# Routing attention and MLP on one core: attention of all sequences as one part, the MLP as a second, steps in pairs

## The chip, the core and the metric

The kernel runs on one core of a Trainium2 chip. The metric is the time of one execution on the device in microseconds. A core has TensorE (PE: matmuls, and PEld: its weight loads), VectorE (DVE), ScalarE (ACT), GpSimd (POOL) and SyncE (SP), which here only issues transfers. Each engine takes the instructions of its own queue in order and waits on semaphores for the others.

## What is computed

Two blocks follow each other. The first is attention with routing, for 4 sequences of 768 tokens and 8 heads of 64: each query and key goes to the nearest of 16 centroids of its head, and a query sees only keys of its own centroid. The second is an MLP on rows of 512 (the 8 heads side by side) with a layer norm and a residual.

```python
q_assign = np.argmax(np.einsum('bhsd,hcd->bhsc', q_n, c_n), axis=-1)
k_assign = np.argmax(np.einsum('bhsd,hcd->bhsc', k_n, c_n), axis=-1)
mask = q_assign[:, :, :, None] == k_assign[:, :, None, :]
scores = np.where(mask, scale * np.matmul(q, k.transpose(0, 1, 3, 2)), -1000000000.0)
attn = softmax(scores)          # over the keys
x = np.matmul(attn, v)          # heads side by side: (4, 768, 512)
...
xn = (x - mu) / np.sqrt(var + 1e-06) * g_ln
out = x + np.maximum(xn @ w_ch1, 0.0) @ w_ch2     # 512 -> 2048 -> 512
```

The two weight matrices come as float64; the kernel turns them into float32 on the chip.

## The kernel before, in words

Two heads make a pair; 4 sequences of 4 pairs give 16 pairs `n`. A pair has two halves `g` of 384 queries and six key tiles `c` of 128: 12 steps of (pair, half, key tile), 192 in all.

One step is `scores` and `weigh`. `scores` (L300) computes, for both heads, the product of the one-hot centroid tiles in bf16 (L307, keys scaled so that a mismatch gives a huge negative number) and adds the float32 product of keys and queries (L312); the heads use different row halves of the array. ScalarE takes the exponential into one of four `e` tiles (L317). `weigh` (L320) multiplies `e` with V, each head on its own column half, and adds over the six key tiles in one PSUM tile (L327). A float32 matmul shows as two instructions in the trace. The sums of `e` over the key tiles, for the denominators, are five additions a half: GpSimd two (L339, L341), VectorE three (L339, L343, L344).

A pair is prepared while the one before it is in its steps: transposes of q and k (L232, copies at L238 and L240), similarities to the centroids (L250, twelve matmuls with q or k as the stationary tile and 32 columns each), routing on VectorE (L260 to L273), and transposes of the one-hot tiles (L285, copies at L291).

`finish` (L350) closes a half in three parts, 2, 5 and 9 steps after it: part 0 copies the accumulator to `xT` and sums the denominators over partitions by a matmul with ones (L361), copies them (L365) and spreads two rows over 64 partitions each by a transfer (L367); part 1 takes the reciprocal (L372), writes it to DRAM (L374) and reads it back broadcast (L377); part 2 multiplies on GpSimd (L384).

The weights come in 32 chunks of 128 x 512 float64 (16 of each matrix), with two buffers. `split_weight` (L176) has ScalarE scale the low words (L184) and VectorE rebuild the high words in five operations (L186 to L197); `join_weight` multiplies and adds on GpSimd (L204, L205). After four chunks of the first matrix `center_w1` subtracts the mean over rows (L212 on TensorE, L216 on VectorE). Chunks of the first matrix begin every fourth step from step 0, those of the second every step from step 64.

The MLP of a sequence is cut into units: for each of two halves of rows, 16 `hidden` (four matmuls of 384 columns and a ReLU: L417, L425), three `rows` (transposes L401, copies, statistics L406) and `project` (48 matmuls of 512 columns, L434; VectorE scales and adds the residual, L445; store at L449). From step 70 on a budget gains 78 a step and pays 48 for a unit, which is then put among the steps; the units of the last sequence come after all steps. So the attention of sequences 1 to 3 stands interleaved with the MLP of 0 to 2.

The program writes this order down in Python; the framework then orders each engine's queue from it, by priority and readiness in a schedule of its own, and adds the waits. All loads and stores of the loop are on SyncE's queue.

A last part tests that all reciprocals lie in a safe range; where they don't, a slow general path (not run here) computes all again.

## Time and profile before

| | us |
|---|---|
| median of 3 runs | 1256.71 (1255.5 to 1257.78) |
| the profiled execution | 1256.49 |
| its span in the trace | 1254.7 |
| TensorE busy | 1176.9 |
| VectorE busy | 373.0 |
| ScalarE busy | 337.5 |
| GpSimd busy | 251.5 |

The span is from the first to the last instruction in the trace; the execution's own time has 1.8 us more. A busy time is the union of an engine's instructions; for TensorE it says nothing of how full the array is, nor at which clock it ran, so the granted clock (PEclk, 1.00 for 2.4 GHz, 0.50 for 1.2) is read beside it. Durations in the trace overlap a little where instructions follow each other; the chain of waits gives each stretch of time to one of them.

### The profile page before, as it was taken

To read this page: it belongs to the slowest core of one execution; us is meant where nothing else is said; L and a number is where in the kernel's file an instruction comes from. 1 tells how busy PE (TensorE), PEld (TensorE's weight loads), DVE (VectorE), ACT (ScalarE), POOL (GpSimd) and SP (SyncE) were. 2 spreads that over 40 slices of the span, in tenths; PEclk is the share of its full clock that TensorE was granted. 3 is DMA by queue.
4 is the path that set the end of the run, shared out by engine and by line. 5 is a ranking of instruction groups with operands and counts; after the bars stand their busy time and mean duration, and the time that the engine had idled before them with its cause. 6 is when DMAs were issued, how large, how long until landed. Compare 5 with 4: busy or idle time off the path is not lost.

```text
span 1254.7 us, 11868 instructions
## 1 busy us (share of the span) xinstructions
PE 1176.9 (94%) x4738; PEld 554.8 (44%) x4738; DVE 373.0 (30%) x562; ACT 337.5 (27%) x532; POOL 251.5 (20%) x188
## 2 busy tenths in 40 slices
PE   6676766999999999999999999999999999999997
PEld 4232322444544455445444554445444443554553
DVE  6999998441221202111120021222111010100010
ACT  3333323443241233122402241142311331120110
POOL 4566766231111011101101010120101011000000
PEclk9787787999999999999999999999999999999999
DMA  7343532221011010020110101110010000000000
GB/s 179 91 134 92 129 103 66 51 51 39 13 29 39 15 26 19 24 53 1 32 27 24 32 13 28 49 33 20 7 36 8 8 7 24 15 1 17 9 9 19
DMA packets 98909, 49.31 MB, mean 39 GB/s; under 512 B 87584, under 2 KB 91680, under 8 KB 98848
## 3 DMA queue, kind: packets, MB, share of 16 engines
q1 hardware_dynamic: 98176, 48.45, 14.8%
q8 instruction: 39, 0.64, 0.2%
q14 instruction: 22, 0.18, 0.0%
q10 hardware_dynamic: 672, 0.03, 0.0%
HBM read 41.98 MB, written 6.39 MB: 39 GB/s over the span
## 4 chain that ended last, share of the span: by engine, by line
PE 82%; DVE 12%; issue 2%; DMA 1%; POOL 1%; SPq 1%; ACT 0%; DVEq 0%; POOLq 0%; ACTq 0%
PE h_ps L417 27%; PE o_ps L434 27%; PE a_ps L327 10%; PE s_ps L312 8%; PE s_ps L307 3%; PE sim_ps L250 3%; DVE ta L189 2%; DVE ta L194 2%; DVE tb L193 2%; PE den_ps L361 2%; DVE ta L186 2%; PE qk_ps L232 1%; DMA raw<-in_moe_w_ch_dram 1%; PE x_ps L401 1%; PE oh_ps L285 1%
## 5 line engine op out<-in xcount | busy, mean ns | idle before, releaser
L417 PE MATMUL h_ps<-xT,w 128*128 128x384 f32 x1024 | 346.7, 492 | 0.0
L434 PE MATMUL o_ps<-w,hT 128*128 128x512 f32 x768 | 342.7, 599 | 0.0
L417 PEld LDWEIGHTS h_ps<-xT,w 128*128 128x128 f32 x1024 | 189.7, 190 | 156.2 <-issue 34.8
L317 ACT ACTIVATE e<-s_ps 128x768 f32<-128x768 f32 x192 | 155.3, 810 | 258.2 <-PE s_ps L312 258.1
L434 PEld LDWEIGHTS o_ps<-w,hT 128*128 128x128 f32 x768 | 141.8, 190 | 187.4 <-issue 187.3
L327 PE MATMUL a_ps<-e,v_sb 128*64 128x384 f32 x768 | 177.6, 543 | 46.1 <-ACT e L317 29.3
L312 PE MATMUL s_ps<-t,t 64*128 64x384 f32 x768 | 165.6, 511 | 0.0
L425 ACT ACTIVATE hT<-h_ps 128x384 f32<-128x384 f32 x128 | 62.9, 491 | 349.5 <-PE h_ps L417 349.5
L339 POOL TENSOR_TENSOR es<-e 128x768 f32<-128x768 f32 x32 | 58.8, 1838 | 370.5 <-ACT e L317 370.5
L327 PEld LDWEIGHTS a_ps<-e,v_sb 128*64 128x64 f32 x768 | 39.8, 141 | 159.5 <-issue 55.7
L384 POOL TENSOR_TENSOR xT<-xT,rb 128x384 f32<-128x384 f32 x32 | 36.8, 1149 | 258.0 <-DMA rb<-row 254.8
L341 POOL TENSOR_TENSOR es<-es,e 128x768 f32<-128x768 f32 x32 | 60.6, 1893 | 138.7 <-ACT e L317 138.7
L372 DVE RECIPROCAL rdens<-rdens 128x6 f32<-128x6 f32 x32 | 6.0, 188 | 231.6 <-DMA rdens<-dsb 231.5
L312 PEld LDWEIGHTS s_ps<-t,t 64*128 64x128 f32 x768 | 73.8, 201 | 0.0
L445 DVE SCALAR_TENSOR_TENSOR o_sb<-o_ps,rstd,xr 128x512 f32<-128x512 f32 x24 | 18.0, 750 | 186.3 <-PE o_ps L434 177.3
L307 PE MATMUL s_ps<-m,m 64*128 64x384 bf16 x384 | 67.2, 347 | 0.1
L204 POOL TENSOR_TENSOR low<-low,tb 128x512 f32<-128x512 f32 x32 | 47.1, 1471 | 68.5 <-DVE tb L197 61.1
L307 PEld LDWEIGHTS <-m 64*128 64x128 bf16 x384 | 18.5, 93 | 93.3 <-issue 90.7
L343 DVE TENSOR_TENSOR es<-es,e 128x768 f32<-128x768 f32 x32 | 32.9, 1027 | 82.7 <-ACT e L317 82.7
L339 DVE TENSOR_TENSOR es<-e 128x768 f32<-128x768 f32 x32 | 35.2, 1101 | 52.8 <-ACT e L317 52.7
L250 PEld LDWEIGHTS sim_ps<-cT,t 128*128 128x128 f32 x384 | 47.3, 200 | 7.8 <-issue 5.0
L184 ACT ACTIVATE low<-raw 128x512 f32<-128x512 uint32 x32 | 21.8, 680 | 99.8 <-POOL w L205 81.7
(78 smaller groups left out, 676.0 us busy)
## 6 DMA issues: line engine op xcount, KB each, us to landing
raw<-in_moe_w_ch_dram SPq DMA_DIRECT2D x32, 512.0 KB, 3.9
q_sb<-in_q_dram SPq DMA_DIRECT2D x32, 192.0 KB, 3.7
k_sb<-in_k_dram SPq DMA_DIRECT2D x32, 192.0 KB, 3.3
v_sb<-in_v_dram SPq DMA_DIRECT2D x32, 192.0 KB, 3.3
rb<-row SPq DMA_DIRECT2D x64, 96.0 KB, 2.8
out_dram<-o_sb SPq DMA_DIRECT2D x24, 256.0 KB, 2.0
rdens<-dsb SPq DMA_DIRECT2D x64, 1.5 KB, 1.8
row<-rdens SPq DMA_DIRECT2D x32, 3.0 KB, 1.4
```

Of the source, the lines that this page charges most:

```text
L204: nc.gpsimd.tensor_tensor(low, low, fb, ALU.mult)
L250: nc.tensor.matmul(sv[:, c, side, :], st[side][:, c * P : (c + 1) * P], cT[:, pr, :, :].rearrange("p j c -> p (j c)"), start=True, stop=True,)
L307: nc.tensor.matmul(s[:, j, :HC], st["m", 1][rows[j], keys], st["m", 0][rows[j], cols], start=True, stop=False,)
L312: nc.tensor.matmul(s[:, j, :HC], st[1][rows[j], keys], st[0][rows[j], cols], start=False, stop=True,)
L317: nc.scalar.activation(e, s[:, :, :HC], AF.Exp, scale=SCALE)
L327: nc.tensor.matmul(acc[j * D : (j + 1) * D, :HC], loaded[n]["v"][:, c, j, :], e[:, j, :], start=(c == 0), stop=(c == NT - 1),)
L339: eng.tensor_tensor(es[c], soft.pop(i - 1), soft.pop(i), ALU.add)
L341: nc.gpsimd.tensor_tensor(es[1], es[1], soft.pop(i), ALU.add)
L384: nc.gpsimd.tensor_tensor(x, x, late.pop((n, g)), ALU.mult)
L417: nc.tensor.matmul(hp[:, :HC], w1[:, c, f * P : (f + 1) * P], xT[:, c, r * HC : (r + 1) * HC], start=(c == 0), stop=(c == NDC - 1),)
L425: nc.scalar.activation(hT, hp[:, :HC], AF.Relu)
L434: nc.tensor.matmul(op, st["hT", r, f][:, tt * P : (tt + 1) * P], w2[:, f, :], start=(f == 0), stop=(f == NFC - 1),)
```

## The change

The attention of all 16 pairs is now one part, whose pools are closed before the MLP of all four sequences runs as a second, with all eight PSUM banks and 20 hidden tiles. The four `xT` tiles stay in SBUF. The bodies of `rows`, `hidden` and `project` are the same; they are no longer cut into units.

- Steps go in pairs (slots, six to a head pair): the scores of the two steps of the next slot, then the weightings of the two of this one. There are five `e` tiles.
- Similarities: the centroids are the stationary tile, and q and k stream, 384 columns at a time, in four matmuls on four column groups of 32 (`tile_position`); ScalarE copies the result, three transposes bring it to tokens on partitions, and the routing has two operations for the one-hots where there were four.
- `finish` works on a pair: four matmuls on four column groups of 32 for the denominators, four rows to spread, one reciprocal, one trip through DRAM, one product. The accumulator of a half is copied to `xT` right behind its last weighting.
- The sums of `e` (five a half, in place), the product with the reciprocals, and all seven operations of the weight conversion are on VectorE; ScalarE's `low` and GpSimd's part are gone. A conversion has one set of work tiles. Two chunks are converted per pair, over all 16 pairs.
- The product of `mean` with g moves from ScalarE to VectorE at the start; q and k have one load buffer each, as before, and are loaded further ahead.

The diff, cut to what the text speaks of:

```diff
+    xpool = ctx.enter_context(tc.tile_pool(name="xpool", bufs=1))
...
-    loads = pool("loads", 2)
+        return stage.enter_context(tc.tile_pool(name=name, bufs=bufs, **kw))
+
+    loads = pool("loads", 1)
     heads = pool("heads", 2)
-    route = pool("route", 2)
+    route = pool("route", 1)
     attn = pool("attn", 2)
-    xpool = pool("xpool", 2)
+    conv = pool("conv", 1)
     dram = pool("dram", 4, space=bass.MemoryType.DRAM)
     ps_s = pool("ps_s", 2, space=PSUM)
     ps_a = pool("ps_a", 1, space=PSUM)
-    ps_t = pool("ps_t", 3, space=PSUM)
-    pools = {}
+    pools = {"t": pool("ps_t", 3, space=PSUM)}
...
-    ones = const.tile([P, D], F32, name="ones")
+    ones = const.tile([P, Q], F32, name="ones")
...
-        oh = const.tile([P, NT, 2, D], BF16, name=f"onehot_{side}")
+        oh = const.tile([P, TH, NHALF, 2, D], BF16, name=f"onehot_{side}")
...
-    DE = HC // D
-    rdens = const.tile([P, B * NPAIR * NHALF, DE], F32, name="rdens")
+    DE = HC // Q
+    rdens = const.tile([P, B * NPAIR, DE], F32, name="rdens")
...
-    for c in range(NDC):
-        nc.scalar.mul(mean[:, c, :], mean[:, c, :], g_sb[:, c : c + 1])
...
+    for c in range(NDC):
+        nc.vector.tensor_scalar_mul(mean[:, c, :], mean[:, c, :], g_sb[:, c : c + 1])
...
     def load_weight(m):
-        src, _ = weight_chunk(m)
-        raw = pools["conv"].tile([P, WC], mybir.dt.int64, tag="raw", name="raw")
-        nc.sync.dma_start(out=raw, in_=src)
-        raws[m] = raw
-
-    halves = {}
+        if m < NWC:
+            raw = conv.tile([P, WC], mybir.dt.int64, tag="raw", name="raw", bufs=2)
+            nc.sync.dma_start(out=raw, in_=weight_chunk(m)[0])
+            raws[m] = raw
...
     def split_weight(m):
-        words = raws.pop(m).bitcast(U32).rearrange("p (n w) -> p n w", w=2)
-        lo, hi = words[:, :, 0], words[:, :, 1]
-        cpool = pools["conv"]
-        ta = cpool.tile([P, WC], U32, tag="ta", name="ta")
-        tb = cpool.tile([P, WC], U32, tag="tb", name="tb")
-        fa, fb = ta.bitcast(F32), tb.bitcast(F32)
-        low = cpool.tile([P, WC], F32, tag="low", name="low")
-        nc.scalar.activation(low, lo, AF.Copy, scale=2.0 ** -52)
+        words = raws[m].bitcast(U32).rearrange("p (n w) -> p n w", w=2)
+        hi = words[:, :, 1]
+        ta = conv.tile([P, WC], U32, tag="ta", name="ta")
+        tb = conv.tile([P, WC], U32, tag="tb", name="tb")
...
-
         nc.vector.tensor_single_scalar(tb, hi, 0x7FF00000, op=ALU.bitwise_and)
+        halves[m] = (ta, tb)
+
+    def join_weight(m):
+        lo = raws.pop(m).bitcast(U32).rearrange("p (n w) -> p n w", w=2)[:, :, 0]
+        ta, tb = halves.pop(m)
+        fa, fb = ta.bitcast(F32), tb.bitcast(F32)
+
         nc.vector.scalar_tensor_tensor(
             out=fa, in0=tb, scalar=float(0x38100000), in1=fa, op0=ALU.is_ge, op1=ALU.mult
         )
+
         nc.vector.tensor_single_scalar(tb, ta, 0xFF800000, op=ALU.bitwise_and)
-        halves[m] = (fa, fb, low)
-
-    def join_weight(m):
-
-        _, dst = weight_chunk(m)
-        fa, fb, low = halves.pop(m)
-        nc.gpsimd.tensor_tensor(low, low, fb, ALU.mult)
-        nc.gpsimd.tensor_tensor(dst, low, fa, ALU.add)
+        nc.vector.scalar_tensor_tensor(
+            out=fb, in0=lo, scalar=2.0 ** -52, in1=fb, op0=ALU.mult, op1=ALU.mult
+        )
+        nc.vector.tensor_tensor(weight_chunk(m)[1], fb, fa, ALU.add)
...
+    def prep_sims(n):
+
...
         sim = ps("sim_ps")
-        sv = sim[:, : NG * NCL].rearrange("p (t s c) -> p t s c", s=2, c=2 * NCL)
-        for c in range(NT):
-            for side in range(2):
+        for side in range(2):
+            for g in range(NHALF):
+                r = (side * NHALF + g) * Q
                 nc.tensor.matmul(
-                    sv[:, c, side, :],
-                    st[side][:, c * P : (c + 1) * P],
+                    sim[r : r + Q, :HC],
                     cT[:, pr, :, :].rearrange("p j c -> p (j c)"),
+                    prepared[n][side][:, g * HC : (g + 1) * HC],
                     start=True,
                     stop=True,
-                )
-        sims = sim[:, : NG * NCL].rearrange("p (g c) -> p g c", c=NCL)
+                    tile_position=(0, r),
+                )
+        sim_sb = route.tile([P, HC], F32, tag="sim", name="sim_sb")
+        nc.scalar.copy(sim_sb, sim[:, :HC])
+        prepared[n]["sim"] = sim_sb
+
+    def prep_route(n):
+        sim_sb = prepared[n]["sim"]
+        simT = ps("simT_ps")
+        for c in range(TH):
+            nc.tensor.transpose(
+                simT[:, c * P : (c + 1) * P], sim_sb[:, c * P : (c + 1) * P], ident
+            )
...
-        first = route.tile([P, NT, 2, 2], F32, tag="first", name="first")
-        nc.vector.tensor_reduce(first.rearrange("p t s j -> p (t s j)"), hit, AX.X, ALU.max)
-        revs = rev.unsqueeze(1).to_broadcast([P, NT, NCL])
+        first = route.tile([P, TH, 2, NHALF * 2], F32, tag="first", name="first")
+        nc.vector.tensor_reduce(first.rearrange("p c s a -> p (c s a)"), hit, AX.X, ALU.max)
+        shape = [P, TH, NHALF * 2, NCL]
 
         for side, op in ((0, ALU.is_equal), (1, ALU.not_equal)):
-            for j in range(2):
-                nc.vector.tensor_tensor(
-                    onehots[side][:, :, j, :NCL],
-                    revs,
-                    first[:, :, side, j].unsqueeze(2).to_broadcast([P, NT, NCL]),
-                    op,
-                )
+            nc.vector.tensor_tensor(
+                onehots[side].rearrange("p c g j d -> p c (g j) d")[:, :, :, :NCL],
+                rev.unsqueeze(1).unsqueeze(1).to_broadcast(shape),
+                first[:, :, side, :].unsqueeze(3).to_broadcast(shape),
+                op,
+            )
...
-    x_of = {}
...
+    xT = [xpool.tile([P, NDC, S], F32, name=f"xT{b}") for b in range(B)]
...
-        e = attn.tile([P, 2, HC], F32, tag="e", name="e", bufs=4)
+        e = attn.tile([P, 2, HC], F32, tag="e", name="e", bufs=5)
...
-        es = sums.setdefault((n, g), {})
-        if c == 1 or c == 3:
-            es[c] = attn.tile([P, 2, HC], F32, tag=f"es{c}", name=f"es{c}")
-            eng = nc.gpsimd if c == 1 else nc.vector
-            eng.tensor_tensor(es[c], soft.pop(i - 1), soft.pop(i), ALU.add)
-        elif c == 4:
-            nc.gpsimd.tensor_tensor(es[1], es[1], soft.pop(i), ALU.add)
-        elif c == 5:
-            nc.vector.tensor_tensor(es[3], es[3], soft.pop(i), ALU.add)
-            nc.vector.tensor_tensor(es[3], es[3], es[1], ALU.add)
+        if c == 1:
+            es = attn.tile([P, 2, HC], F32, tag="es", name="es", bufs=3)
+            sums[n, g] = es
+            nc.vector.tensor_tensor(es, soft.pop(i - 1), soft.pop(i), ALU.add)
+        elif c > 1:
+            es = sums[n, g]
+            nc.vector.tensor_tensor(es, es, soft.pop(i), ALU.add)
+        if c == NT - 1:
+            b, pr = pairs[n]
+            nc.scalar.copy(xT[b][:, pr, g * HC : (g + 1) * HC], accs.pop((n, g))[:, :HC])
...
-    def finish(n, g, part):
+    def finish(n, part):
...
         if part == 0:
-            if b not in x_of:
-                x_of[b] = xpool.tile([P, NDC, S], F32, tag="x", name="xT")
-            nc.scalar.copy(x_of[b][:, pr, cols], accs.pop((n, g))[:, :HC])
-            es = sums.pop((n, g))[3]
             den = ps("den_ps")
             for j in range(2):
-                nc.tensor.matmul(
-                    den[j * D : (j + 1) * D, :HC], ones, es[:, j, :], start=True, stop=True
-                )
-            dsb = attn.tile([P, HC], F32, tag="dsb", name="dsb")
-            nc.scalar.copy(dsb[: D + 1, :], den[: D + 1, :HC])
-            for j in range(2):
-                nc.sync.dma_start(
-                    out=rdens[j * D : (j + 1) * D, r, :],
-                    in_=dsb[j * D : j * D + 1, :],
-                )
+                for g in range(NHALF):
+                    r = (j * NHALF + g) * Q
+                    nc.tensor.matmul(
+                        den[r : r + Q, :HC], ones, sums[n, g][:, j, :],
+                        start=True, stop=True, tile_position=(0, r),
+                    )
+            dsb = attn.tile([P, HC], F32, tag="dsb", name="dsb", bufs=1)
+            nc.scalar.copy(dsb, den[:, :HC])
+            for r in range(0, P, Q):
+                nc.sync.dma_start(out=rdens[r : r + Q, n, :], in_=dsb[r : r + 1, :])
         elif part == 1:
-            nc.vector.reciprocal(rdens[:, r, :], rdens[:, r, :])
-            row = dram.tile([2, HC], F32, tag="row", name="row")
-            nc.sync.dma_start(out=row.rearrange("j (p e) -> (j p) e", e=DE), in_=rdens[:, r, :])
-            rb = attn.tile([P, HC], F32, tag="rb", name="rb")
+            nc.vector.reciprocal(rdens[:, n, :], rdens[:, n, :])
+            row = dram.tile([2, S], F32, tag="row", name="row")
...
+            rb = attn.tile([P, S], F32, tag="rb", name="rb", bufs=1)
...
                 nc.sync.dma_start(
                     out=rb[j * D : (j + 1) * D, :],
-                    in_=row[j : j + 1, :].to_broadcast([D, HC]),
-                )
-            late[n, g] = rb
+                    in_=row[j : j + 1, :].to_broadcast([D, S]),
+                )
+            late[n] = rb
         else:
-            x = x_of[b][:, pr, cols]
-            nc.gpsimd.tensor_tensor(x, x, late.pop((n, g)), ALU.mult)
...
+            x = xT[b][:, pr, :]
+            nc.vector.tensor_tensor(x, x, late.pop(n), ALU.mult)
...
-    prep = {
-        0: lambda n: prep_transpose(n, 0),
-        2: lambda n: prep_transpose(n, 1),
-        4: prep_route,
-        9: prep_onehot,
-    }
-    for s in sorted(prep):
-        prep[s](0)
-    load(1, "qk")
-    work = deque()
-    pools["ffn"] = pool("ffn", 2)
-    conv = fast.enter_context(ExitStack())
-    pools["conv"] = conv.enter_context(tc.tile_pool(name="conv", bufs=2))
...
-    begin = {4 * m if m < NW1 else seq + 16 + m - NW1: m for m in range(NWC)}
-    join = {i + (2 if m < NW1 else 1): m for i, m in begin.items()}
-    MLP0 = seq + 22
+    slots = per // 2
+    for side in range(2):
+        prep_transpose(0, side)
+        load(1, "qk"[side])
+    prep_sims(0)
+    prep_route(0)
+    prep_onehot(0)
+    prep_transpose(1, 0)
+    load(2, "q")
     load_weight(0)
+    load_weight(1)
     scores(0)
-    due = {}
-    units = 0
-    for i in range(len(steps)):
-        n, step = divmod(i, per)
-        if step == 1 and n + 1 < len(pairs):
+    scores(1)
+    for u in range(len(pairs) * slots):
+        n, slot = divmod(u, slots)
+        nxt = n + 1 < len(pairs)
+        if slot == 1:
             load(n + 1, "v")
-        for what in due.pop(i, ()):
-            finish(*what)
-        if n + 1 < len(pairs) and step in prep:
-            prep[step](n + 1)
-            if step == 2 and n + 2 < len(pairs):
-                load(n + 2, "qk")
-        if i + 1 < len(steps):
-            scores(i + 1)
-        if i in begin:
-            m = begin[i]
-            if m + 1 < NWC:
-                load_weight(m + 1)
+        if slot == 0 and nxt:
+            prep_transpose(n + 1, 1)
+            load(n + 2, "k")
+        if slot == 1 and nxt:
+            prep_sims(n + 1)
+        if slot == 2 and nxt:
+            prep_route(n + 1)
+        if slot == 4 and nxt:
+            prep_onehot(n + 1)
+        if slot == 5 and n + 2 < len(pairs):
+            prep_transpose(n + 2, 0)
+            load(n + 3, "q")
+        if slot == 1 and n:
+            finish(n - 1, 0)
+        for i in (2 * u + 2, 2 * u + 3):
+            if i < len(steps):
+                scores(i)
+        weigh(2 * u)
+        weigh(2 * u + 1)
+        if slot == 3 and n:
+            finish(n - 1, 1)
+        if slot == 5 and n:
+            finish(n - 1, 2)
+        m = 2 * n + slot // 3
+        if slot % 3 == 0:
             split_weight(m)
-        weigh(i)
-        if i in join:
-            m = join[i]
+        elif slot % 3 == 1:
             join_weight(m)
-            if m < NW1 and m % NDC == NDC - 1:
-                center_w1(m // NDC)
-            if m + 1 == NWC:
-                conv.close()
-                pools["rows"] = pool("rows", 2)
-        _, g, c = steps[i]
-        if c == NT - 1:
-            for part, wait in enumerate((2, 5, 9)):
-                due.setdefault(i + wait, []).append((n, g, part))
-
-        if i >= seq and i % seq == 10:
-            work.extend(moe_units(i // seq - 1))
-        if i >= MLP0:
-            units += 78
-            while work and units >= seq:
-                work.popleft()()
-                units -= seq
-            units = min(units, seq)
-    for i in sorted(due):
-        for what in due[i]:
-            finish(*what)
-    work.extend(moe_units(B - 1))
-    while work:
-        work.popleft()()
+            load_weight(m + 2)
+        elif m < NW1 and m % NDC == NDC - 1:
+            center_w1(m // NDC)
+    for part in range(3):
+        finish(len(pairs) - 1, part)
...
+    stage.close()
+    pools["t"] = pool("ps_m", 8, space=PSUM)
+    ffn = pool("ffn", 2)
...
+        hT = ffn.tile([P, HC], F32, tag="hT", name="hT", bufs=NFC + 4)
+        nc.scalar.activation(hT, hp[:, :HC], AF.Relu)
...
+    for b in range(B):
+        for r in range(NHALF):
+            hTs = [hidden(b, r, f) for f in range(NFC)]
+            x, rstd = rows(b, r)
+            for tt in range(TH):
+                project(b, r, tt, hTs, x, rstd)
+
     flag = all_in_range()
```

## Rows read from the trace of the kernel before

**Rows 1.** The page's first part: busy us of each engine, share of the span, instructions.
```profile
PE 1176.9 (94%) x4738; PEld 554.8 (44%) x4738; DVE 373.0 (30%) x562; ACT 337.5 (27%) x532; POOL 251.5 (20%) x188
```
**Rows 2.** Windows: us, busy time of each engine (instructions), PEclk, DMA share, GB/s.
```profile
23.00:262.00 239.00, 180.34 (x918) 73.89 (x920) 207.97 (x251) 87.84 (x134) 141.07 (x91) 0.83 0.36 94
262.00:1080.00 818.00, 817.97 (x3298) 383.92 (x3295) 140.60 (x251) 222.40 (x347) 102.64 (x66) 1.00 0.10 25
```
**Rows 3.** VectorE lines: count, duration ns min/median/max, first and last start, shapes.
```profile
L193 DVE TENSOR_SCALAR tb<-raw x32: 410/1302/2015, 10.8 to 206.6; 128x512 uint32<-128x512 uint32 x32
L189 DVE SCALAR_TENSOR_TENSOR ta<-raw,ta x32: 676/680/2299, 11.1 to 204.4; 128x512 uint32<-128x512 uint32 x32
L339 DVE TENSOR_TENSOR es<-e x32: 946/959/2022, 37.1 to 1053.3; 128x768 f32<-128x768 f32 x32
L266 DVE TENSOR_TENSOR hit<-hit,rev x16: 545/557/1617, 17.2 to 952.6; 128x384 f32<-128x384 f32 x16
L273 DVE TENSOR_TENSOR onehot_q<-rev,first x32: 244/251/1859, 20.2 to 953.9; 128x96 bf16<-128x96 f32 x32
```
**Rows 4.** The chain of waits from 253 to 276 us: start, us, what, instructions.
```profile
253.85 0.78 PE oh_ps L285 x12
254.63 0.27 PE s_ps L307 x2
254.90 0.65 PE s_ps L312 x4
255.54 0.80 PE a_ps L327 x4
...
259.76 0.80 PE qk_ps L232 x6
...
261.47 0.80 PE a_ps L327 x4
262.27 0.65 PE den_ps L361 x4
...
267.14 3.63 PE mean_ps L212 x8
...
272.48 2.79 PE sim_ps L250 x24
```
**Rows 5.** TensorE's timeline near 254 us: start, us, operation, instructions.
```profile
254.56 0.34 PE L307 MATMUL s_ps<-m,m 64*128 64x384 bf16 x2
254.73 0.81 PE L312 MATMUL s_ps<-t,t 64*128 64x384 f32 x4
```
**Rows 6.** TensorE's timeline from 18 us: the first scores.
```profile
23.06 0.50 PE L307 MATMUL s_ps<-m,m 64*128 64x384 bf16 x2
```
**Rows 7.** The chain of waits from 1163 us: the last half of the MLP.
```profile
1163.63 41.28 PE h_ps L417 x128
1204.91 1.31 PE x_ps L401 x12
1206.22 41.33 PE o_ps L434 x96
```
**Rows 8.** DMA issues (KB each, median us to landing), and one issue on SyncE's timeline.
```profile
raw<-in_moe_w_ch_dram SPq DMA_DIRECT2D x32, 512.0 KB, 3.9
rb<-row SPq DMA_DIRECT2D x64, 96.0 KB, 2.8
rdens<-dsb SPq DMA_DIRECT2D x64, 1.5 KB, 1.8
row<-rdens SPq DMA_DIRECT2D x32, 3.0 KB, 1.4
263.46 1.17 SPq L367 DMA_DIRECT2D rdens<-dsb  x2
```

180 lines of the change are left out of this document (78 added, 102 removed).

## The prediction

> **What bounds the kernel now.** I read the page's totals first. TensorE is busy 1176.9 of 1254.7 us; VectorE 373.0 and ScalarE 337.5 look far from it [rows 1]. That average hides two stages, and the windows part them [rows 2]. From 23 to 262 us, which is sequence 0 and the first weight conversions with almost no MLP work, VectorE is busy 208.0 of 239 us and TensorE only 180.3, at a granted clock of 0.83, a mean of its two levels, 1.2 and 2.4 GHz. From 262 to 1080 us TensorE never stops, at full clock, and VectorE idles 83%. So the first stage belongs to VectorE and the rest to TensorE, and the change must be priced by stage.
>
> Why VectorE is so full is in the durations of its lines [rows 3]. The same masking operation (L193) takes 0.410 us at best and 1.302 in the median; L189 takes 0.676 to 2.299, the sum over two tiles (L339) 0.946 to 2.022. GpSimd is busy 141.1 us of that first window [rows 2], on tiles of its own, and I put the long ones down to it.
>
> For TensorE I read the chain of waits where it runs alone at full clock [rows 4]. One step is 0.27 + 0.65 + 0.80 = 1.72 us: similarity of the one-hots, scores, weighting with V. The 0.65 is two matmuls of two instructions each, side by side: one of the MLP's, as wide and alone, takes 2 x 41.28 / 128 = 0.645 [rows 7]. Where a denominator follows a weighting, both on two column halves of the array, it takes 0.65, while a weighting behind scores takes 0.80; and the first one-hot matmuls take 0.27 in the chain while the scores start 0.17 behind them [rows 5]. So every change between row halves and column halves costs: 0.15 one way, 0.10 the other, 0.25 a step.
>
> **Before, by that price list.** First scores at 23.1 us [rows 6]; 192 steps x 1.72 = 330.2; 15 pairs prepared behind that, each 2 x 0.80 (transposes of q and k) + 2.79 (similarities) + 0.78 (one-hots) = 5.17, so 77.6; 32 denominators at 0.65 to 0.80, say 0.73, 23.4; centering of w1 4 x 3.63 = 14.5 [rows 4]; the MLP 8 halves x (41.28 + 1.31 + 41.33) = 671.4; the end from 1247.6 to 1254.7, 7.2 [rows 7]; outside the span 1256.49 - 1254.7 = 1.8. Sum 1149.2 against 1256.5 profiled (the median of the runs shown, 1256.7, is the same): 107 us are waits and low clock. The first window has 239 - 180.3 = 58.7 us of TensorE idle and 180.3 x 0.17 = 30.7 of clock, 89 of the 107.
>
> **The change part by part.** *Steps in pairs.* Order scores, scores, weighting, weighting: 0.27 + 0.65 + 0.17 + 0.65 + 0.80 + 0.65 = 3.19 for two steps in place of 3.44; 96 x 0.25 = 24.0 us less TensorE. The exponentials get more room, two steps ahead rather than one, and five e tiles rather than four.
>
> *Transposed similarities.* 2.79 goes; four matmuls come in four column groups of 32, and three transposes. The trace has no four groups. Bounds: 0.65 + 0.15 if all run side by side as two do, 4 x 0.65 + 0.15 = 2.75 if none does. I take 0.80, being nearest to the two-group rows. Transposes: 6 cost 0.80 with a switch, 12 cost 1.31, so 0.11 each: 3 x 0.11 + 0.15 = 0.48. Pair: 1.28 against 2.79, 15 x 1.51 = 22.6 less. The new ScalarE copy in between (some 0.5 us, the order of a 384-column operation) has a whole slot of TensorE work, over 3 us, to hide in; without that cover the transposes and all behind them wait.
>
> *Denominators.* One group of four per pair, 0.80, in place of two: 23.4 - 12.8 = 10.6 less; bounds as for the similarities. Together with them the four groups can cost 2 x 1.95 x 16 = 62 us more. The Trainium skill (TensorE: Matmul & The Clock Gate, Part 3) speaks against full overlap: three column groups measured 2.38 times, not three. Carried to four that would be 0.65 x 3 / 2.38 = 0.82, an estimate, some 5 us more in the sum; here two groups give a clean factor of two, and nothing in this trace shows four.
>
> *VectorE takes everything.* GpSimd's five sorts of work and ScalarE's `low` move over. At the price without GpSimd [rows 3]: a chunk is 3 x 0.41 + 3 x 0.68 + one 512-column sum (between 0.56 for 384 and 0.96 for 768, 0.69) = 3.96, two a pair 7.9; ten sums of 768 columns 9.6; two copies and four routing operations at 0.56, 3.3; two one-hot operations of 192 columns, between 0.25 and 0.56, 0.7; reciprocal 0.2; the product with 1/den 0.96. Pair 22.7, 16 pairs 363, centering 16 x 0.68 = 11: 374 us. TensorE needs for the same stage 96 x 3.19 = 306.2, plus 15 x (1.6 + 0.78 + 1.28) = 54.9, 16 x 0.80 = 12.8 and 14.5: 388.4. ScalarE's total for the whole run, MLP included, is less than that [rows 1]: it does not bind.
>
> So both engines are within 4% of each other, and TensorE alone is not the whole answer. VectorE's slots vary: 2.7 to 4.8 us, 7.6 where routing meets the centering, against 3.2 to 4.6 and 7.3 on TensorE. Five e tiles let VectorE lag by about a slot, so most of it evens out. What can stop its queue is the reciprocal, behind four small transfers, and the product, behind two hops through DRAM; behind these stand the sums, behind the sums the e tiles, then exponentials and weightings. Two slots (8 us) are left for each against some 5 [rows 8]. Bounds for the stalls: 0, and both trips wholly exposed (the rival below). I take 20 us, 1.2 a pair, near the low end because the lag allowed exceeds the trips' margin.
>
> *On SyncE*, a pair issues four `dsb` rows, one `row`, two `rb` (before: four, two, four), so three fewer, beside the same six loads and two raw chunks; a raw load waits for the join of the chunk two earlier, and what is behind it is later q, k and v, needed a pair later.
>
> *MLP as a second part.* Its TensorE price stays 671.4; it loses VectorE's company, which it doesn't need. At the border the first hidden tiles need xT of sequence 0, long finished, and freed banks: 0 us, with the last pair's round of some 11 as the other bound. Start: one-hots no longer stand behind half-converted chunks mixed with GpSimd, but there is a hop more: 23.1 kept, 18 to 26 possible.
>
> **Sum.** 23.1 + 388.4 + 671.4 + 7.2 + 1.8 = 1091.9, plus 20: 1112 us.
>
> **Rivals.**
> 1. *TensorE alone binds*, stalls near 0: 1080 to 1100. For it: five e tiles and two slots of room. Against: 96% VectorE load. Chance 0.22; the forecast (1100 to 1130) has 0.40.
> 2. *VectorE becomes the bound*: 27 to 28 us a pair, waits included, so 16 x 3 to 4 us over TensorE's 24: 1140 to 1165; with a lower clock as in the first window [rows 2], 1175. 0.16. The Trainium skill (Perfetto Trace Analysis, Optimizing Scalar/DVE Operations) says a saturated VectorE should give work to ScalarE or GpSimd, which would make this change wrong; it adds that GpSimd may be no help, as the two share a port. The rows bear out the addition.
> 3. *The pairing doesn't happen*: queues are in the framework's order, not the program's (L189 stands above L193 in the program, and yet the first L193 starts at 10.8 us and the first L189 at 11.1 [rows 3]). Then 24.0 stays: 1136. 0.10.
> 4. *Four groups run in turn*: +62, 1174. 0.07.
> 5. *Slower.* VectorE's queue meets both trips unhidden in every pair. Price: denominator 0.8, copy 0.5, four `dsb` 2 x 1.17 to issue and 1.8 to land; then `row` 1.4 and two `rb` 1.2 + 2.8, 10.8 us [rows 8]. 22.7 + 10.8 = 33.5 a pair, 536 in place of 388.4 + 20 = 408, and 11 at the border: 1251. It is slower than before from 33.9 us a pair on, which a landing behind a 512 KB chunk (3.9) passes: 37.4 a pair, some 1313. For it: VectorE had no cover work left between those waits. Against: two slots of room. 0.05.
>
> **Numbers.** Likeliest 1112. Low 1080: rival 1 with the start at its shorter bound and a little less. High 1176: rivals 2 to 4. Left out: rival 5 and the outer parts of 1, 2 and 4, some 0.16. No change (within 0.2%, 2.5 us, about what a measurement of this kernel can tell) lies only in the mild end of rival 5: 0.01; slower 0.04; faster 0.95.
>
> **What would show it.** TensorE over 92% busy from 25 to 430 us with the clock near 1; the first long run of hidden matmuls near 430; pairs some 25.5 us apart; in the chain 0.65 for the second weighting of a pair and about 0.8 for the four-group matmuls; L193's successor flat at 0.41; GpSimd idle; VectorE 85 to 95% busy in the stage. A stage longer than 450 us, with e tiles or one-hots as the releasers of TensorE and VectorE waiting for transfers, would prove the forecast wrong, as would a four-group matmul over 2 us.

## The result, and the profile after

The kernel after takes 1131.9 us (median of 4 runs, 1131.25 to 1133.01) against 1256.82: a ratio of 0.9008, interval 0.8992 to 0.9023. The forecast of 1112 us had sign and range right and its point 20 us too low. Execution times given below without a range are those of a single execution. The page after has these busy times and slices of the span (28.3 us each):

```profile
PE 1076.1 (95%) x4530; PEld 530.5 (47%) x4530; DVE 391.9 (35%) x662; ACT 300.6 (27%) x484; POOL 3.3 (0%) x28
...
PE   5897778999999999999999999999999999999997
...
DVE  6999999966566565000010010010010010010010
...
PEclk8988989999999999999999999999999999999998
```

Against [rows 1] TensorE is busy for 100.8 us less, and the weak slices are fewer. But there is a border within the attention: up to the eighth slice, some 230 us, VectorE is full and TensorE is not; then it is the other way round. The windows, in the columns of [rows 2]:

```profile
23.00:230.00 207.00, 173.22 (x1073) 74.30 (x1071) 200.38 (x347) 88.20 (x128) 0.00 (x0) 0.93 0.44 122
230.00:452.00 222.00, 221.70 (x1524) 98.51 (x1520) 136.21 (x189) 128.05 (x185) 0.00 (x0) 1.00 0.24 58
452.00:1131.00 679.00, 670.72 (x1889) 351.03 (x1889) 40.69 (x89) 78.26 (x162) 0.00 (x0) 1.00 0.03 10
```

In the first, TensorE idles 33.8 us and loses some 12 more to a granted clock of 0.93 (0.07 x 173.2): 46 us. In the second it idles 0.3. The MLP starts at 452.55 us, where the forecast had 431.5 (23.1 + 388.4 + 20), and from there to the end takes 678.7 us, where it had 671.4 + 7.2. So what is off lies before 230 us. There TensorE waits for VectorE (wait, us in total, times, longest):

```profile
PE sim_ps L247 <- DVE t L238: 26.8, 7, 6.3
PE oh_ps L295 <- DVE onehot_q L282: 6.0, 3, 2.5
```

One of these waits in VectorE's timeline (start, us, operation). The similarity matmul needs the copy L238 of 94.49; TensorE stood from 88.98 to 95.09:

```profile
87.54 0.95 DVE L348 TENSOR_TENSOR es<-e 128x768 f32<-128x768 f32 x1
88.41 0.68 DVE L201 SCALAR_TENSOR_TENSOR tb<-raw,tb 128x512 f32<-128x512 uint32 x1
89.12 0.69 DVE L204 TENSOR_TENSOR w<-tb,ta 128x512 f32<-128x512 f32 x1
89.85 0.43 DVE L182 TENSOR_SCALAR ta<-raw 128x512 uint32<-128x512 uint32 x1
90.19 0.42 DVE L188 TENSOR_SCALAR tb<-raw 128x512 uint32<-128x512 uint32 x1
90.53 0.69 DVE L185 SCALAR_TENSOR_TENSOR ta<-raw,ta 128x512 uint32<-128x512 uint32 x1
91.25 0.69 DVE L196 SCALAR_TENSOR_TENSOR ta<-tb,ta 128x512 f32<-128x512 uint32 x1
91.86 2.72 DVE L215 SCALAR_TENSOR_TENSOR w<-w,g_sb,mean_ps 128x512 f32<-128x512 f32 x4
94.49 0.55 DVE L238 COPY t<-qk_ps 128x384 f32<-128x384 f32 x1
```

The transposes that the copy reads had ended at 85.04. Ahead of a 0.55 us copy VectorE then did the seven operations of one chunk, four of the next, a sum of `e` and a centering (2.72 us). The durations are the ones forecast; their place is not. The last operation of a chunk tells when the chunks were done: count, ns min/median/max, first and last start:

```profile
L204 DVE TENSOR_TENSOR w<-tb,ta x32: 677/689/692, 16.6 to 216.2; 128x512 f32<-128x512 f32 x32
```

The program puts two chunks into each of 16 pairs, up to some 450 us. The framework has all 32 done by 217, four to six a pair: 32 chunks in 200 us, while a pair lasts some 33 us there against a TensorE price of 23.3. By the forecast's price (22.7 us a pair with two chunks, 3.96 a chunk) four chunks make 30.6 us of VectorE work.

Where TensorE binds, the chain of waits shows a pair of steps and the four-column-group matmuls:

```profile
320.66 0.78 PE sim_ps L247 x8
321.44 0.65 PE den_ps L367 x8
322.09 0.27 PE s_ps L317 x2
322.36 0.65 PE s_ps L322 x4
323.00 0.16 PE s_ps L317 x2
323.16 0.65 PE s_ps L322 x4
323.81 1.44 PE a_ps L337 x8
325.25 0.48 PE simT_ps L263 x3
...
343.93 0.78 PE sim_ps L247 x8
```

Two steps are 0.27 + 0.65 + 0.16 + 0.65 + 1.44 = 3.17 us, and the next pair's similarities come 23.27 us behind the first.

### The profile page after: what moved, and what is told of

Same layout as the page of the kernel before. It is cut to its first block, busy times and chain, and to the rows that moved or that the text cites. A ratio compares the mean times of both kernels' runs of the same rounds, so it can differ in the third digit from the quotient of the medians.

```text
span 1131.2 us, 11304 instructions
## 1 busy us (share of the span) xinstructions
PE 1076.1 (95%) x4530; PEld 530.5 (47%) x4530; DVE 391.9 (35%) x662; ACT 300.6 (27%) x484; POOL 3.3 (0%) x28
## 4 chain that ended last, share of the span: by engine, by line
PE 80%; DVE 14%; DMA 2%; issue 2%; SPq 1%; ACT 0%; DVEq 0%
PE h_ps L493 29%; PE o_ps L507 29%; PE a_ps L337 7%; PE s_ps L322 6%; DVE es L351 3%; PE s_ps L317 2%; DVE tb L201 2%; DVE ta L196 2%; DVE ta L185 1%; PE qk_ps L230 1%; DVE tb L200 1%; PE sim_ps L247 1%; PE x_ps L478 1%; PE den_ps L367 1%; DVE w L204 1%
## 5 line engine op out<-in xcount | busy, mean ns | idle before, releaser
L493 PE MATMUL h_ps<-xT,w 128*128 128x384 f32 x1024 | 331.7, 486 | 0.6 <-ACT dsb L372 0.6
L507 PE MATMUL o_ps<-w,hT 128*128 128x512 f32 x768 | 330.9, 592 | 0.0
L337 PE MATMUL a_ps<-e,v_sb 128*64 128x384 f32 x768 | 144.8, 499 | 0.0
L351 DVE TENSOR_TENSOR es<-es,e 128x768 f32<-128x768 f32 x128 | 122.2, 955 | 38.9 <-ACT e L327 33.6
L483 DVE BATCH_NORM_STATS2 bn<-xr 128x6 f32<-128x512 f32 x24 | 15.9, 689 | 323.5 <-ACT xr L481 323.5
L247 PE MATMUL sim_ps<-t,cT 128*32 128x384 f32 x128 | 21.9, 526 | 28.7 <-DVE t L238 28.7
L317 PEld LDWEIGHTS <-m 64*128 64x128 bf16 x384 | 18.7, 94 | 47.3 <-issue 32.4
L301 ACT ACTIVATE m<-oh_ps 128x768 bf16<-128x768 bf16 x32 | 24.2, 808 | 28.1 <-PE oh_ps L295 28.1
L390 DVE TENSOR_TENSOR xT<-xT,rb 128x768 f32<-128x768 f32 x16 | 15.3, 956 | 26.0 <-DMA rb<-row 26.0
L236 ACT COPY t<-qk_ps 128x384 f32<-128x384 f32 x32 | 15.3, 478 | 33.5 <-PE qk_ps L230 33.5
L367 PE MATMUL den_ps<-es,ones 128*32 128x384 f32 x128 | 23.8, 600 | 0.3 <-DVE es L351 0.3
```

Of the source, the lines that this page charges most:

```text
L247: nc.tensor.matmul(sim[r : r + Q, :HC], cT[:, pr, :, :].rearrange("p j c -> p (j c)"), prepared[n][side][:, g * HC : (g + 1) * HC], start= ...
L301: nc.scalar.mul(m, t[:, :S], -FAR if side else 1.0)
L317: nc.tensor.matmul(s[:, j, :HC], st["m", 1][rows[j], keys], st["m", 0][rows[j], cols], start=True, stop=False,)
L337: nc.tensor.matmul(acc[j * D : (j + 1) * D, :HC], loaded[n]["v"][:, c, j, :], e[:, j, :], start=(c == 0), stop=(c == NT - 1),)
L351: nc.vector.tensor_tensor(es, es, soft.pop(i), ALU.add)
L367: nc.tensor.matmul(den[r : r + Q, :HC], ones, sums[n, g][:, j, :], start=True, stop=True, tile_position=(0, r),)
```

## The experiments

**1. The conversions spread as the program has them.** `issue_after` keeps the framework from scheduling an instruction ahead of a given one.

```diff
-            nc.vector.tensor_tensor(es, es, soft.pop(i), ALU.add)
+            last[0] = nc.vector.tensor_tensor(es, es, soft.pop(i), ALU.add)
...
-            split_weight(m)
+            with tc.issue_after(last[0].ins):
+                split_weight(m)
...
-            join_weight(m)
+            with tc.issue_after(last[0].ins):
+                join_weight(m)
```

> The changed kernel with each chunk's split and join tied behind the sum of its own slot in VectorE's queue (issue order only, no wait), so that two chunks a pair are converted as the program says, and not four to five a pair early on as its queue has them. Theory (early conversions fill VectorE in the first seven pairs and TensorE waits there; spread, TensorE binds all through): MLP starts near 410 us instead of 452.6, time 1086 to 1100. Rival (an even load of over 90% on VectorE stalls TensorE as much as the uneven one): 1120 to 1135, MLP start after 440.

1090.14 us (1089.48 to 1090.42), ratio 0.8673 (0.8658 to 0.8687). The same instructions, 42 us less than after. Four of the 42 come at the start: the first scores run at 17.18 us instead of 21.13, because no conversion stands between the routing operations of the first pair any more. Line L204, then the windows, then TensorE's one long wait:

```profile
L204 DVE TENSOR_TENSOR w<-tb,ta x32: 691/692/694, 27.5 to 404.0; 128x512 f32<-128x512 f32 x32
```
```profile
23.00:230.00 207.00, 207.00 (x1387) 92.95 (x1383) 187.01 (x299) 113.15 (x165) 0.00 (x0) 1.00 0.42 103
230.00:409.00 179.00, 173.78 (x1187) 76.63 (x1184) 155.81 (x248) 100.78 (x146) 0.00 (x0) 0.99 0.38 95
```
```profile
PE den_ps L368 <- DVE es L352: 4.6, 1, 4.6
```

TensorE does not stop between 23 and 230 us although VectorE is 90% busy there. The theory holds; it was queue order.

**2. The conversion left out**: `split_weight` and `join_weight` empty, the weights set by two GpSimd memsets at the start.

> The changed kernel without the conversion of the weights: the 32 loads stay, the seven VectorE operations a chunk are left out, w1 and w2 are set to constants by GpSimd at the start (so the MLP's numbers are not the reference's). What TensorE needs when VectorE has room. Theory: first scores 21.1, 96 x 3.17 + 15 x 3.66 + 16 x 0.65 + 14.5 = 384, MLP start near 406, time 1084 to 1092, and TensorE over 98% busy between. Rival (something other than the conversions, such as the transfers of the reciprocals or the four-group matmuls, holds the stage up): MLP start above 425, time above 1104.

1112.07 us, with the MLP from 432.4 us on. By these numbers the rival is right, but the edit itself made the miss. VectorE's and GpSimd's timelines at the start:

```profile
4.26 13.39 DVE L139 TENSOR_SCALAR c_sb<-c_sb,c_tmp 128x64 f32<-128x64 f32 x1
```
```profile
3.80 6.93 POOL L153 MEMSET w<- 128x8192 f32 x1
10.66 6.93 POOL L154 MEMSET w<- 128x8192 f32 x1
```

A 128x64 operation beside the memsets lasts until the second of them is over, so the first scores came at 29.26 us instead of 21.13. Raw loads, which no reader held back any more, ran into the small transfers; once VectorE's reciprocal waited 14.7 us and TensorE 11.8 behind it. That is the slower rival's mechanism (5), once. From 200 us to the MLP TensorE stood for 0.4 us in all. The run says nothing on conversions alone.

**3. The two copies that TensorE waited for, moved to ScalarE.**

```diff
-                nc.vector.tensor_copy(t_sb[:, g * HC : (g + 1) * HC], t[:, :HC])
+                nc.scalar.copy(t_sb[:, g * HC : (g + 1) * HC], t[:, :HC])
```

> The changed kernel with the second copy of each q and k transpose on ScalarE in place of VectorE, the copy that TensorE waits for longest (28.7 us at the similarities). Theory (VectorE is full in the first half, and this wait is only where TensorE meets it): VectorE loses two copies of 0.55 in each of some seven pairs, 6 to 9 us, time 1122 to 1127. Rival (the copy's place in VectorE's queue is the cause): the wait of 28.7 goes whole, time 1100 to 1106.

1133.78 us, neither: nothing was gained. The wait moved to the next thing behind the conversions:

```profile
PE oh_ps L295 <- DVE onehot_q L282: 34.1, 6, 7.5
```

The releaser that a wait names is only the last link. What stands ahead of it in its queue was the cause, and VectorE, with 193.81 of 207 us busy from 23 to 230, had as much of it.

**4. The kernel before, with GpSimd's work and `low` on VectorE**, and nothing else of the change.

```diff
-        nc.scalar.activation(low, lo, AF.Copy, scale=2.0 ** -52)
...
-        halves[m] = (fa, fb, low)
+        halves[m] = (fa, fb, lo)
...
-        nc.gpsimd.tensor_tensor(low, low, fb, ALU.mult)
-        nc.gpsimd.tensor_tensor(dst, low, fa, ALU.add)
+        nc.vector.scalar_tensor_tensor(
+            out=fb, in0=low, scalar=2.0 ** -52, in1=fb, op0=ALU.mult, op1=ALU.mult
+        )
+        nc.vector.tensor_tensor(dst, fb, fa, ALU.add)
...
-            eng = nc.gpsimd if c == 1 else nc.vector
...
-            nc.gpsimd.tensor_tensor(x, x, late.pop((n, g)), ALU.mult)
+            nc.vector.tensor_tensor(x, x, late.pop((n, g)), ALU.mult)
```

> The kernel before with only the move to VectorE: the joins and the scaling of the low words as in the changed kernel, the two GpSimd sums and the product on VectorE, everything else as it was. Theory (most of the gain is not the end of the contention, since VectorE takes over as much work as it gains in speed): 32 x 3.96 + 11 for weights and 5.8 pairs at 15.4 make 227 us of VectorE where 208 of 239 were busy, so 5 to 20 us less, time 1236 to 1252. Rival (contention with GpSimd was what held the first stage): the 59 us of TensorE's idle time in the first window go, time near 1198 to 1215.

1190.95 us, 66 less than before: my theory fell and the gain went past the rival's. The window from 23 to 200 us, first of the kernel before, then of this one:

```profile
23.00:200.00 177.00, 126.40 (x600) 50.25 (x601) 173.73 (x206) 62.34 (x97) 115.80 (x76) 0.80 0.42 114
```
```profile
23.00:200.00 177.00, 157.88 (x922) 67.09 (x922) 169.00 (x318) 70.99 (x103) 0.00 (x0) 0.95 0.47 123
```

VectorE is as busy in both but finishes 318 instructions in place of 206, 0.53 us each in place of 0.84. The mask operation that took 1.302 us in the median [rows 3] (L193 there):

```profile
L191 DVE TENSOR_SCALAR tb<-raw x32: 415/420/426, 10.5 to 221.1; 128x512 uint32<-128x512 uint32 x32
```

All VectorE operations that the two kernels share, on the same shapes, last 89.6 us longer in the kernel before: the five of a chunk 153.2 us against 83.8, the sums 102.1 against 91.6, the routing 32.1 against 22.4. That is 0.56 us for each of GpSimd's 160 instructions there.

But this edit takes away a second thing as well. The waits of the kernel before between 23 and 262 us:

```profile
ACT low L184 <- POOL w L205: 81.7, 24, 8.6
PE a_ps L327 <- ACT e L317: 29.3, 12, 4.8
PE a_ps L327 <- ACT xT L357: 16.7, 5, 4.9
PE den_ps L361 <- DVE es L344: 12.5, 4, 8.1
```

Of TensorE's 58.7 us of idle time there, 46.0 are waits for ScalarE, and ScalarE stood 81.7 us for GpSimd's last operation of a chunk, with `low` at the head of its queue and the exponentials and copies behind it (run 5 shows the same wait again). GpSimd in its turn waited 61.1 us in the whole run for VectorE's last operation of a chunk. Run 4 has no `low`: its TensorE idles 19.1 us in that window, 18.7 of them for VectorE's sums. So the 66 us are a faster VectorE and a ScalarE that no longer waits for GpSimd, together; no run parts the two.

From here to the kernel after it is 59 us, near the 57 that the forecast's three TensorE terms make; that is a difference between two kernels, not those terms by themselves.

**5. The end of the conversion on GpSimd again, in the spread kernel.**

```diff
-        nc.vector.scalar_tensor_tensor(
-            out=fb, in0=lo, scalar=2.0 ** -52, in1=fb, op0=ALU.mult, op1=ALU.mult
-        )
-        nc.vector.tensor_tensor(weight_chunk(m)[1], fb, fa, ALU.add)
+        low = conv.tile([P, WC], F32, tag="low", name="low")
+        nc.scalar.activation(low, lo, AF.Copy, scale=2.0 ** -52)
+        nc.gpsimd.tensor_tensor(low, low, fb, ALU.mult)
+        nc.gpsimd.tensor_tensor(weight_chunk(m)[1], low, fa, ALU.add)
```

> The spread version (two chunks a pair) with the last two operations of a chunk back where they were before: ScalarE scales the low words, GpSimd multiplies and adds. VectorE loses 2 x 0.69 us a chunk, 44 us in all; GpSimd gets 64 operations of some 1.4 us, 90 us. Theory (each us in which GpSimd has its operands takes VectorE's second port away, as the kernel before against its VectorE-only version showed): VectorE's load returns to about TensorE's, stalls come back, 1096 to 1115, and the masking operations (0.42 us each) again show a maximum above 1.3. Rival (the contention matters only where VectorE is already full): 1088 to 1092.

1209.82 us: 120 more, but not by the theory. ScalarE waits, and TensorE behind it:

```profile
ACT low L202 <- POOL w L204: 135.6, 31, 7.3
```
```profile
PE s_ps L318 <- ACT e L328: 68.9, 25, 5.7
```

There is one `low` tile; its next writing waits for GpSimd, with the exponentials queued behind it. The masking operation, for which the theory wanted a maximum above 1.3 us, takes 0.425 at most. The run shows what a wait on a queue that others need costs; VectorE, busy for only 276.5 of the 457 us from 23 to 480, says little on shared access. Runs 10 and 11 ask that question without a wait.

**6. The pairing undone, in the spread kernel.**

```diff
-        for i in (2 * u + 2, 2 * u + 3):
-            if i < len(steps):
-                scores(i)
-        weigh(2 * u)
-        weigh(2 * u + 1)
+        for i in (2 * u, 2 * u + 1):
+            if i + 2 < len(steps):
+                scores(i + 2)
+            weigh(i)
```

> The spread version with steps one by one again: scores, weighting, scores, weighting, the scores still two steps ahead. Theory (each change between row and column halves costs 0.10 or 0.15 us, one pair of changes a step instead of one for two steps): 96 x 0.25 = 24 us more, 1112 to 1117, with 0.80 for each weighting in the chain. Rival (the change of halves hides behind loads of the next weights when TensorE is not short of work): 1090 to 1096.

1106.41 us, 16.3 more, between the two. The chain has 0.27 + 0.65 + 0.80 = 1.72 us a step, as priced. Run 9 explains the missing 8 us: the spread kernel has a wait at the end of its attention that this one mostly lacks (1.1 us). Against run 9, which lacks it too, this is 23.4 us slower; 96 x 0.25 = 24.0 was forecast.

**7. Twelve token-major similarity matmuls, in the spread kernel**, as in the kernel before (L250), with no copy and no transposes.

```diff
-                nc.tensor.matmul(
-                    sim[r : r + Q, :HC],
...
-                    tile_position=(0, r),
-                )
...
+                    nc.tensor.matmul(
+                        sv[:, c, side, g, :],
+                        prepared[n][side][:, o : o + P],
+                        cT[:, pr, :, :].rearrange("p j c -> p (j c)"),
...
```

> The spread version with the similarities as before: twelve matmuls with q or k as the stationary tile and 32 columns each, no copy, no three transposes. Theory: 2.79 in place of 0.78 + 0.48 in each of 15 pairs, and the denominators no longer beside a matmul of the same column groups, 0.13 more: 15 x 1.53 + 2 = 25 us more, 1112 to 1118. Rival (the copy and the transposes on the way cost as much as the matmuls saved, or the twelve hide under weight loads): 1088 to 1098.

1123.02 us, 32.9 more. The chain has 2.79 for them, and 0.78 for the denominators, which now switch column groups on their own: 15 x 1.53 + 16 x 0.13 = 25.0 us, as priced (1.53 is 2.79 less 0.78 and 0.48). The rest is the start, 1.9 us later (first scores at 19.08), and the clock: without any wait of TensorE the granted clock was 0.83 in the windows 103 to 113, 213 to 223 and 343 to 353 us and 0.95 and 0.88 in the two from 153 to 173. In these four pairs it fell within a microsecond behind the twelve narrow matmuls. That is some 6.8 us. Run 1 has no such dip there.

**8. One copy a chunk instead of seven operations**, in the order of the kernel after (the weights are then not the reference's).

```diff
+        hi = raws.pop(m).bitcast(F32).rearrange("p (n w) -> p n w", w=2)[:, :, 1]
+        nc.vector.tensor_copy(weight_chunk(m)[1], hi)
```

> The changed kernel (conversions where its queue has them) with one VectorE copy of the high words per chunk in place of the seven operations, so the weights and the MLP's numbers are not the reference's; loads and order as they were. It asks the question of the run without conversion again, without the constants written by GpSimd at the start and with loads that wait for a reader. Theory (the conversions alone hold the stage up): first scores near 21, MLP start 403 to 410, time 1083 to 1092. Rival (something else in the stage does too): MLP start above 420.

1108.27 us, with the MLP from 428.1 us on, as the rival has it: without most of the conversions' work something still holds the stage up. VectorE is only 123.06 of 207 us busy from 23 to 230, and TensorE waits all the same. VectorE's waits from 23 to 430 us, then TensorE's:

```profile
DVE w L182 <- DMA raw<-in_moe_w_ch_dram: 35.8, 28, 2.5
```
```profile
PE sim_ps L225 <- DVE t L216: 13.4, 3, 6.4
```

Scheduled early, the copies reach the head of the queue before their chunks are loaded and hold what is behind them. All the work spread (run 1) takes 1090; a seventh of the operations, unspread, takes 1108. Here the place in the queue cost more than the amount of work.

**9. The last wait of the spread kernel.** In run 1, VectorE stood 3.42 us for a broadcast, with pair 15's last four additions behind it:

```profile
399.33 0.96 DVE L391 TENSOR_TENSOR xT<-xT,rb 128x768 f32<-128x768 f32 x1 [3.42 <-DMA rb<-row]
400.20 2.02 DVE L352 TENSOR_TENSOR es<-es,e 128x768 f32<-128x768 f32 x2
```

```diff
-        if slot == 5 and n:
+        if slot == 5 and n and nxt:
             finish(n - 1, 2)
...
-    for part in range(3):
+    finish(len(pairs) - 1, 0)
+    with tc.issue_after(last[0].ins):
+        finish(len(pairs) - 2, 2)
+    for part in range(1, 3):
         finish(len(pairs) - 1, part)
```

> The spread version, with the reciprocal's multiply of pair 14 moved behind the last additions of pair 15. In the spread run VectorE stood 3.42 us for that pair's broadcast (L391) with the last four additions queued behind it, and TensorE then waited 4.6 us at the last denominators (L368). It is the slower rival's mechanism, once. Theory (that wait is the cause of the 4.6): the wait falls to under 1 us, the first MLP matmul comes near 404.5 instead of 408.81, and the time is 1084.5 to 1087.5 against 1090.1. Rival (the four additions were late anyway, for the last chunk of weights ahead of them): the wait stays above 3 us and the time is 1089 to 1091.

1083.0 us (1081.89 to 1083.13), ratio 0.8622 (0.861 to 0.8634), the fastest version here. The wait is gone and the MLP starts at 403.56 us. It gained 7.1 us for a wait of 4.6 (1084.5 at the least was expected), because the wait also cost clock. The same first stretch of the MLP, run 1 and then this one:

```profile
409.00:415.00 6.00, 6.00 (x14) 3.41 (x15) 1.19 (x6) 0.00 (x0) 0.00 (x0) 0.72 0.03 2
```
```profile
403.00:409.00 6.00, 5.44 (x17) 3.32 (x18) 1.19 (x6) 0.48 (x1) 0.00 (x0) 1.00 0.03 2
```

The first hidden half takes 43.26 us there and 41.55 here.

**10 and 11. GpSimd work by itself, in the spread kernel**: two (run 11: four) additions behind each chunk into a tile that nobody reads.

```diff
+        for _ in range(2):
+            own = conv.tile([P, WC], F32, tag="own", name="own")
+            nc.gpsimd.tensor_tensor(own, weight_chunk(m)[1], weight_chunk(m)[1], ALU.add)
```

> The spread version, with two additions of 128x512 on GpSimd behind each weight chunk, 64 in all, into a tile that nobody reads; the result is the reference's. They read the finished chunk, so they come one pair of additions per 10 us or so. No instruction of VectorE waits for a result of them (the centring of w1 writes over what they have read, one slot later). Theory (GpSimd's elementwise work holds VectorE by itself): at 1.3 to 1.45 us each, as the kernel before and the clean part of the joins-on-GpSimd run have them, 64 of them are 83 to 93 us in which VectorE's operations last longer or stand; VectorE's 350 busy us of the 391 us attention become 430 or more, and the time is 1115 to 1160. In the trace the additions of 128x768, 0.955 us otherwise, have a mean of 1.1 us or more. Rival (the 66 us that came back with GpSimd's work on VectorE were waits between the two engines and not shared access): 1088 to 1093, and the 0.955 us stay.

> The same with four additions behind each chunk, 128 in all, about 170 us of GpSimd work in the attention (the kernel before has some 240 us of it in 1.2 times the time). Theory (GpSimd holds VectorE): VectorE would need 350 and 170 of the 391 us, so the attention lasts 500 to 530 us and the kernel 1200 to 1240. Rival (no shared access): 1088 to 1095.

1106.28 us (ratio 0.8808, 0.8794 to 0.8821) and 1136.64 us: 16 and 46 us more. The direction is the theory's, the size is not. VectorE's lines in runs 10 and 11, where 0.955 and 0.42 us are normal:

```profile
L355 DVE TENSOR_TENSOR es<-es,e 128x768 f32<-128x768 f32 x128 | 142.9, 1116 | 6.7
L352 DVE TENSOR_TENSOR es<-e 128x768 f32<-128x768 f32 x32 | 37.2, 1161 | 0.0
```
```profile
L355 DVE TENSOR_TENSOR es<-es,e 128x768 f32<-128x768 f32 x128 | 144.3, 1128 | 7.3 <-ACT e L331 0.6
L352 DVE TENSOR_TENSOR es<-e 128x768 f32<-128x768 f32 x32 | 37.1, 1159 | 0.0
L182 DVE TENSOR_SCALAR ta<-raw 128x512 uint32<-128x512 uint32 x32 | 26.8, 837 | 0.0
L188 DVE TENSOR_SCALAR tb<-raw 128x512 uint32<-128x512 uint32 x32 | 26.8, 837 | 0.0
L279 DVE TENSOR_TENSOR hit<-hit,rev 128x384 f32<-128x384 f32 x16 | 19.4, 1214 | 0.6
```

In run 10 the additions are 142.9 + 37.2 in place of 122.2 + 30.4 us: 27.5 us for 64 GpSimd instructions, 0.43 each, and not the whole 1.62 that one of them lasts. Run 11 has 28.8 us more in the additions, 26.7 in L182 and L188, and 12.3 in the routing (L279, 19.4 in place of 8.9, and a one-hot): 67.8 for 128, 0.53 each. VectorE's busy time says the same: 393.0 us in run 1, 419.8 and 460.1 here. So GpSimd's work lengthens VectorE's with no wait between them; I had counted every GpSimd instruction as lost to VectorE in full. The price is no constant: it was 0.43 and 0.53 here and 0.56 in the kernel before, and in run 5, where VectorE had room, the additions grew by 1.7 us in all.

The Trainium skill (SBUF — State Buffer, in the section on who interferes with whom) says that VectorE and GpSimd share one pair of ports, which whoever comes first keeps for a whole instruction, and that only some forms of VectorE instruction meet it, among them those with two inputs in SBUF while GpSimd reads SBUF. Run 2 agrees (13.39 us for an operation that takes 0.25 in the kernel after). Run 11 agrees that it is certain operations that are hit: while GpSimd works from 140.16 to 145.92 us, the product of two SBUF tiles (L279) takes 1.25 us in place of 0.56, and L275 beside it, with one input from PSUM, keeps its 0.56. L201 and L204, which fall where GpSimd waits, keep their 0.69.

## Why the forecast was right, and where it failed

*The stage argument held, with a link missing.* The gain came from the waits of the first window and from TensorE's own work. "I put the long ones down to it", GpSimd, is shown by runs 4, 10 and 11. "So the first stage belongs to VectorE" passes over the path: by the waits under run 4, TensorE stood there mostly for ScalarE, ScalarE for GpSimd and GpSimd for VectorE, and how much of run 4's 66 us each link is worth stays open.

*TensorE's terms held.* Pairing: 3.17 against 3.19 for two steps, and 23.4 of 24.0 us by run 6 against run 9. Similarities: 0.78 and 0.48 against 0.80 and 0.48. Four column groups run side by side: eight instructions in 0.65 us, as two groups did [rows 4], so rival 4 is out. The Trainium skill's factor of 2.38 for three groups (TensorE: Matmul & The Clock Gate, Part 3), carried to four, gave an estimate of 0.82; the trace does not bear that out. The denominators came cheaper, 0.65 against 0.80, because they follow the similarities on the same groups. A pair is 23.27 us against 6 x 3.19 + 1.60 + 0.78 + 1.28 + 0.80 = 23.6.

*VectorE's prices held* for one operation, 0.42, 0.69 and 0.955 us, flat, but not their sum. It was 374 us for the attention; in run 1 VectorE is busy 345.3 us from 17 to 409, since recorded durations overlap (in the timeline above L188 starts 0.34 us behind L182, which is recorded at 0.43). So an even queue asks some 10% less of VectorE than of TensorE, and not the 4% on which "96% VectorE load" rests. What held too is the MLP with its end, 678.7, the border (0.6 us), and the start (first scores at 21.13 us, inside 18 to 26).

*The step that failed* is "most of it evens out", with its 20 us of stalls: the attention took 452.55 - 21.13 = 431.4 us against a TensorE price of 388.4, so 43 more. I compared totals for the stage, 374 against 388.4, at "two a pair". But the framework puts a queue in its own order, and conversions need only a loaded chunk and a free tile, so it drew them forward to four to six a pair. The first half of the attention was bound by VectorE and the second left it 39% idle. Rival 3 rested on this very fact, and I applied it only to the order of scores and weightings, which came out as in the program. Run 1 restores the even spread and gives 1090.1 us, near the forecast's sum without stalls (1091.9). In part that is luck: the start is 5.9 us shorter than the 23.1 of the sum and the attention, 391.6 us, 3.2 longer. The 20 us were a wrong guess on both sides, 43 for the kernel as it is and about 3 for an even queue.

The signs set out in advance say the same. From 25 to 430 us TensorE was busy 91.7% at a clock of 0.97 (over 92% and near 1 were expected) and VectorE 79.8% (85 to 95); pairs came some 33 us apart and then mostly 23.3 (25.5 expected); the stage ran past 450 us, with one-hots among the releasers, though VectorE waited for transfers only 1.3 us between 23 and 230. The time lies in the range because the range is wide: 1131.9 is 2 us outside the 1100 to 1130 of the forecast itself.

*The rivals.* 1 is what the spread kernel does. 2 (by its own terms 1140 to 1156, not 1165) named the right engine for the wrong reason: not some 28 us in every pair, but some 32 in the first six or seven (230 - 21 = 209 us, with 222 / 23.3 = 9.5 pairs left behind them). The Trainium skill's advice quoted there, to take work off a full VectorE, is given only as something that may make sense. Followed, it would have led the wrong way here: giving VectorE GpSimd's work and `low` took 66 us off (run 4). 3 did not happen: the chain has the steps in pairs. 5 did not happen; VectorE's waits for the two trips sum to 28 us from 23 to 452, mostly covered. It showed once in run 2 and once, as 3.42 us, at the end of run 1.

In sum: 1256.8, less 66 without GpSimd's part and `low` (run 4), less 59 with the rest of the change, makes 1131.9; less 42 with the conversions spread, less 7 with the last multiply out of the way, makes 1083.0.

## What to carry to other kernels

When work is moved to an engine that a stage needs to 90% or more, price it by stretch, in the order in which the queue will hold it, and not by the stage's total: work that is ready early is drawn forward and stands ahead of what is urgent. Read from the trace where the first and the last of the moved instructions start, and tie background work to a late instruction of its slot where that isn't where you meant it. And look for what stands ahead of a wait's releaser before moving the releaser.

## What was not expected of the hardware

Two GpSimd memsets of 6.93 us held a small VectorE operation until both were over, 13.39 us (run 2). Elementwise work on GpSimd into a tile that nobody reads cost VectorE 0.43 us an instruction at 64 and 0.53 at 128 (runs 10 and 11). Four column groups of 32 ran in the time of two of 64, 0.65 us. A wait of 4.6 us on TensorE was followed by a granted clock of 0.72 over the 6 us from 409 us on (run 1), a mean of its two levels, 1.2 and 2.4 GHz; and in run 7 it fell with no wait at all behind twelve matmuls of 32 columns, in four pairs of 15.
